# Adding the two halves of the attended values inside the transposing product on TensorE

## The chip, the core and the metric

The kernel runs on one core of a Trainium2 chip. The metric is device time of one launch in microseconds (us); the number given for a version is the median of its runs. The engines are named as in the profile: PE (TensorE's matrix products), PEld (its loads of the stationary operand), DVE (VectorE), ACT (ScalarE), POOL (GpSimd), SP (SyncE, which here only issues transfers).

## What is computed

Causal attention with a compressive memory over 4 batches of 8 heads, 576 tokens of 64 values each, feeds a layer of 8 experts of which each of the 2304 tokens goes to one.

```python
scores = scale * np.matmul(q, k.transpose(0, 1, 3, 2)); scores = np.where(causal, -1e9, scores)
a = np.exp(scores - scores.max(-1, keepdims=True)); a /= a.sum(-1, keepdims=True) + 1e-09
local = np.matmul(a, v)
mem_out = np.einsum('bhsd,bhde->bhse', phi(q), M_prev) / mem_norm
attn = g * mem_out + (1 - g) * local                 # B, H, S, D -> x of (B*S, H*D)
logits = x @ w_gate + modality_bias[modality_id]; e_idx = np.argmax(logits, axis=1)
for e in range(E):                                    # gate_w: the softmax value of the chosen expert
    out[mask_e] = gate_w[mask_e, None] * (np.maximum(x[mask_e] @ w1[e], 0.0) @ w2[e])
```

## The kernel before

**Precision.** Most matrix products are made of several in a reduced form of fp32 (`F32R`): an operand is split into a high and a low part, both of which are multiplied. The values `v` of a head lie in `vhl` as 64 columns of high parts beside 64 columns of low parts. With them as stationary operand (`av`, L707) the product of attention weights (`pth`, `ptl`) and values comes out in PSUM with 128 rows: 64 rows from the high parts and 64 from the low ones, one column a token. The attended value of a head is the sum of these halves.

**A head's way.** There are 32 heads, two to a pair, four pairs to a batch. `scores` (L641) gives the scores by TensorE, DVE masks them and takes the maximum (L669), ACT takes exponentials (L675); `ptrans` (L686) turns the result by TensorE transposes, ACT and DVE split it (L701, L703); `av` multiplies it with the values. The product lies in two PSUM banks, one of the first 128 tokens and one of the other 448. `memory` (L749) makes the memory's part of a pair by an fp32 product (L758).

**The sum of the halves, before.** For two of four heads (`NAVP = 2`) ACT copies both halves out (L733 to `ot`, L735 to `avt`), and POOL adds them in place (L744). For the other two ACT copies the lower half to `avt` (L738), and DVE adds the upper half from PSUM (L740). `ot` collects a pair, 64 rows a head. `combine` (L778) then brings tokens to the rows: five TensorE transposes of 128 columns a pair (L794), in two PSUM banks of three and two blocks, which DVE multiplies by the softmax's divisor (L797); POOL adds the memory's part (L801).

**What follows.** After each batch `gate` (L804) turns x and multiplies it with the gate's weights, `route` (L844) and `rank` (L925) choose experts on DVE and scatter the tokens' numbers to tables by POOL (L920). An expert's work is cut into slots of up to 256 or 384 tokens: `fetch` (L1002) reads the table by SP (L1009) and gathers rows by POOL (L1016); `slot` (L1032) turns them (L1042), splits them (L1050, L1052), and makes the first (L1064) and second product (L1086), with ACT (L1073) and DVE (L1075) between. The first three slots belong to the most frequent expert of batch 0 and run among the attention's work; slot 3 takes the tokens that this expert has left over, slot 4 more of them, and the others belong to a second expert, whose weights come by SP (L978) and are split by ACT (L985) and DVE (L989) once the attention's buffers are free.

**What sets the order.** Every step is an operation of a planner (`Plan`, L57) with an engine, an assumed duration and a place in the program's loop over heads. The planner goes through assumed time, and on each engine takes, of the steps that could begin within `WINDOW` ns of the earliest, the one with the lowest priority number; `EARLIER` shifts that number by stage and engine. Each engine runs its list strictly in this order. So a change of a duration, a window or a shift can move steps anywhere in the program.

Of the kernel before, what the change touches and what calls it, by code (L numbers as in the profile page):

```python
# [212 lines left out]
def kernel(  # L213
# [71 lines left out]
    NAVP = 2  # L285
# [12 lines left out]
    Plan.WINDOW = dict(zip(("PE", "ACT", "DVE", "POOL", "SP"), (0, 80, 85, 135, 75)))  # L298

    EARLIER = {  # L300
        "av": (-240.75, -614.75, 695.5, -837, 0),
        "bet": (0, 0, 0, 0, -366),
        "c": (-412, 0, 147.25, -2057.75, 0),
        "con": (0, 0, 0, 0, -347.25),
        "e": (222.75, -57, 141.25, 334, 0),
        "e1": (189.75, -20.5, -235.75, 614.5, 0),
        "e2": (186, 1704, -359, -1036.25, 0),
        "f": (0, 0, 1086.5, -188, 1075),
        "f1": (0, 0, -1054, -169.75, 612.5),
        "f2": (0, 0, 779.75, -443.5, -1457.5),  # L310
        "g": (-100, -1024, -307.5, 0, 1315),
        "k": (-396.5, -421.75, -279.25, 0, -133.25),
        "l": (0, 0, 33.25, 0, 0),
        "l2": (0, 0, 217.5, 0, 0),
        "ld": (0, 0, 0, 0, 204.5),
        "m": (418, 232, 747.75, 90.5, 0),
        "pt": (-80.25, 236.75, -864, 0, 0),
        "q": (-1459.5, 812.75, -363, 451.75, -995.5),
        "r": (85, -318.5, 476, 905, 0),
        "sc": (-53.75, 1043, 452, 0, 0),  # L320
        "tab": (0, 0, 0, 0, 200.25),
        "v": (0, 0, 0, -729, 0),
        "w": (0, 1380.25, 0, 286.25, -1110),
        "w1": (0, 179.25, 848.5, 0, 301.75),
        "w2": (0, -77, -1205.5, 0, 42.25),
        "warm": (-247, 0, 0, 0, 0),
# [58 lines left out]
    avt = ring(ap_, "avt", 1, [P, S])  # L385
    ot = ring(ap_, "ot", 2, [P, S])
# [12 lines left out]
    def setup():  # L399
# [13 lines left out]
        def pads():  # L413
# [293 lines left out]
    def av(d, prio):  # L707
# [21 lines left out]
        o_, a_ = ot[p % 2][64 * hh:64 * hh + 64], avt[0][64 * hh:64 * hh + 64]  # L729
# [47 lines left out]

    def combine(p, prio):  # L778
        b, h0 = divmod(p * 2, H)
        o_, m_, x_ = ot[p % 2], mt[0], xb[0]  # L780

        def e0():
            nc.vector.scalar_tensor_tensor(out=rnd, in0=nden[:, p % 4], scalar=1.0e-9,
# [541 lines left out]
    o = 0  # L1325
# [96 lines left out]
```

## Time and profile before

| | |
|---|---|
| median of three runs (lowest to highest) | 554.32 us (549.8 to 556.81) |
| the profiled execution: its own time | 550.81 us |
| its span, from first to last instruction | 549.1 us |
| busy share of the span: PE, PEld, DVE, ACT, POOL | 91%, 81%, 60%, 60%, 46% |
| mean granted TensorE clock | 0.966 of full speed |

Times within the profile count from the start of its span. A busy PE is not a PE at its peak: products overlap, and the length that the profile gives to one is several times the step to the next. The attention lasts until about 310 us; the change from the first expert to its leftovers and to the second one falls between 340 and 380, and the rest is the experts' products.

### The profile page before, as it was taken

To read this page: it belongs to the slowest core of one execution; us is meant where nothing else is said; L and a number is where in the kernel's file an instruction comes from. 1 tells how busy PE (TensorE), PEld (TensorE's weight loads), DVE (VectorE), ACT (ScalarE), POOL (GpSimd) and SP (SyncE) were. 2 spreads that over 40 slices of the span, in tenths; PEclk is the share of its full clock that TensorE was granted. 3 is DMA by queue.
4 is the path that set the end of the run, shared out by engine and by line. 5 is a ranking of instruction groups with operands and counts; after the bars stand their busy time and mean duration, and the time that the engine had idled before them with its cause. 6 is when DMAs were issued, how large, how long until landed. Compare 5 with 4: busy or idle time off the path is not lost. (4 is left out here: it accounts for less than half of the span.)

```text
span 549.1 us, 10861 instructions
## 1 busy us (share of the span) xinstructions
PE 497.9 (91%) x3420; PEld 445.1 (81%) x3420; DVE 330.5 (60%) x1066; ACT 329.0 (60%) x923; POOL 251.9 (46%) x257
## 2 busy tenths in 40 slices
PE   8898899987899889979898999769999999999992
PEld 8787888875787778869897898769897987989891
DVE  3788788897798988988878336653315512313010
ACT  4798898986999979979298244333325513222110
POOL 8462984656788768865761062350030004010100
PEclk9799899999899989989899999979999999999997
DMA  5888887988777997953740025474036203000100
GB/s 96 189 206 169 206 201 182 231 189 154 192 176 198 238 189 191 220 164 95 180 110 3 20 61 180 78 233 146 18 96 182 83 19 88 29 19 21 40 0 36
DMA packets 97101, 70.43 MB, mean 128 GB/s; under 512 B 73936, under 2 KB 74320, under 8 KB 97042
## 3 DMA queue, kind: packets, MB, share of 16 engines
q1 hardware_dynamic: 93330, 59.99, 45.2%
q0 software_dynamic: 3712, 9.72, 5.8%
q8 instruction: 28, 0.46, 0.4%
q14 instruction: 31, 0.25, 0.2%
HBM read 32.36 MB, written 10.16 MB: 77 GB/s over the span
## 5 line engine op out<-in xcount | busy, mean ns | idle before, releaser
L675 ACT ACTIVATE P<-P,nm 128x576 f32<-128x576 f32 (+4 forms) x160 | 88.5, 558 | 9.1 <-DVE nm L669 6.0
L1024 POOL DMA_INDIRECT out_dram<-osb,ids x19 | 18.9, 997 | 156.0 <-ACT osb L1093 115.3
L1064 PE MATMUL pa<-xh,w1h 128*128 128x256 f32 (+2 forms) x288 | 84.4, 293 | 2.6 <-ACT xh L1050 2.6
L1064 PE MATMUL pa<-xl,w1h 128*128 128x256 f32 (+2 forms) x288 | 83.4, 290 | 0.5 <-DVE xl L1052 0.3
L1064 PE MATMUL pa<-xh,w1l 128*128 128x256 f32 (+2 forms) x288 | 83.1, 288 | 0.0
L1075 DVE SCALAR_TENSOR_TENSOR hlo<-pa,hh 128x256 fp32r<-128x256 f32 (+1 forms) x72 | 29.8, 416 | 69.8 <-ACT hh L1073 69.7
L703 DVE TENSOR_TENSOR ptl<-pa,pth 128x512 fp32r<-128x512 f32 (+1 forms) x128 | 65.6, 564 | 3.0 <-ACT pth L701 2.4
L1073 ACT ACTIVATE hh<-pa 128x256 fp32r<-128x256 f32 (+1 forms) x80 | 29.0, 367 | 61.1 <-PE pa L1064 54.2
L669 DVE CUSTOM_DVE_ANT_0 P<-pa,maskw 128x320 f32<-128x320 f32 (+3 forms) x160 | 62.2, 427 | 4.2 <-PE pa L657 3.5
L684 PE MATMUL pa<-ident,P 128*128 128x128 f32 x320 | 57.6, 285 | 4.0 <-ACT P L675 3.7
L657 PE MATMUL pa<-ks,qs 128*128 128x192 f32 (+3 forms) x186 | 55.5, 329 | 5.9 <-ACT avt L735 2.9
L1086 PE MATMUL pa<-w2h,hh 128*128 128x512 f32 (+1 forms) x152 | 60.4, 397 | 0.0
L701 ACT ACTIVATE pth<-pa 128x512 fp32r<-128x512 f32 (+1 forms) x128 | 57.0, 511 | 5.0 <-PE pa L684 4.4
L1086 PE MATMUL pa<-w2l,hh 128*128 128x512 f32 (+1 forms) x152 | 59.6, 392 | 0.0
L1064 PEld LDWEIGHTS pa<-xh,w1h 128*128 128x128 f32 x288 | 55.6, 193 | 3.4 <-ACT xh L1050 2.9
L1064 PEld LDWEIGHTS pa<-xl,w1h 128*128 128x128 f32 x288 | 55.6, 193 | 1.2 <-DVE xl L1052 0.9
L1086 PE MATMUL pa<-w2h,hlo 128*128 128x512 f32 (+1 forms) x144 | 56.5, 392 | 0.0
L1064 PEld LDWEIGHTS pa<-xh,w1l 128*128 128x128 f32 x288 | 55.5, 193 | 0.0
L1093 ACT ACTIVATE osb<-pa,ids 128x512 f32<-128x512 f32 (+1 forms) x19 | 13.1, 687 | 68.4 <-PE pa L1086 63.1
L657 PE MATMUL pa<-kls,qs 128*128 128x192 f32 (+3 forms) x186 | 49.2, 295 | 0.4 <-DMA kls<-kl 0.4
L684 PEld LDWEIGHTS pa<-ident,P 128*128 128x128 f32 x320 | 40.4, 147 | 6.3 <-ACT P L675 6.0
L684 PE MATMUL pa<-swp,P 128*128 128x128 f32 x160 | 39.5, 287 | 6.1 <-DVE kl L617 2.5
(234 smaller groups left out, 1198.9 us busy)
## 6 DMA issues: line engine op xcount, KB each, us to landing
ks<-kh SPq DMA_DIRECT2D x62, 144.0 KB, 3.0
kls<-kl SPq DMA_DIRECT2D x62, 144.0 KB, 3.4
raw<-in_moe_w_dram SPq DMA_DIRECT2D x32, 256.0 KB, 3.5
qn<-in_q_dram SPq DMA_DIRECT2D x32, 144.0 KB, 4.3
kn<-in_k_dram SPq DMA_DIRECT2D x32, 144.0 KB, 4.2
qs<-qh SPq DMA_DIRECT2D x31, 144.0 KB, 2.6
qs<-ql SPq DMA_DIRECT2D x31, 144.0 KB, 2.7
vn<-in_v_dram SPq DMA_DIRECT2D x32, 128.0 KB, 3.0
```

What stands on the lines that cost most here:

```text
L657: nc.tensor.matmul(t.ap[0:m, o:o + z - x], lhsT=l[:, QS[j]:QE[j]], rhs=r[:, x:z], start=(i == 0), stop=(i == len(terms) - 1))
L669: nc.vector.tensor_tensor_reduce(out=pj[:, x:z], in0=t.ap[0:m, o:o + z - x], in1=mk, scale=-1.0, scalar=nm if x else 3.0e38, op0=ALU.add, ...
L675: g.op("ACT", act_ns(w, False, 2), lambda pj=pj, nm=nm, den=den, w=w: nc.scalar.activation(out=pj[:, 0:w], in_=pj[:, 0:w], func=AF.Exp, sc ...
L684: nc.tensor.transpose(t[:, o:o + P], prow[c % NPB][j][:, kb * P:(kb + 1) * P], swp if j == kb else ident)
L701: g.op("ACT", act_ns(n), lambda t=t, o=o, n=n: nc.scalar.activation(out=hi[:, o:o + n], in_=t.ap[:, 0:n], func=AF.Copy), r=[t], w=[("ph_", ...
L703: g.op("DVE", dve_ns(n), lambda t=t, o=o, n=n: nc.vector.tensor_tensor(out=lo[:, o:o + n], in0=t.ap[:, 0:n], in1=hi[:, o:o + n].bitcast(F3 ...
L1024: g.op("POOL", 1310, lambda: nc.gpsimd.indirect_dma_start(out=out[:, :], out_offset=bass.IndirectOffsetOnAxis(ap=ids[u % 4][0:m, t, 0:1].b ...
L1064: nc.tensor.matmul(hp.ap[:, 0:n_], lhsT=a[:, c, f * P:(f + 1) * P], rhs=x_[:, c, 0:n_], start=(n == 0), stop=(n == 3 * KC - 1))
L1073: g.op("ACT", act_ns(z - a), lambda f=f, hp=hp, i=i, a=a, z=z: nc.scalar.activation(out=hh[i][:, f, 0:z - a], in_=hp.ap[:, a:z], func=AF.R ...
L1075: g.op("DVE", dve_ns(z - a), lambda f=f, hp=hp, i=i, a=a, z=z: nc.vector.scalar_tensor_tensor(out=hlo[i][:, f, 0:z - a], in0=hp.ap[:, a:z] ...
L1086: nc.tensor.matmul(op.ap[0:m], lhsT=a[:, f, ts], rhs=w_[:, f], start=(y == 0 and n == 0), stop=(y == 3 and n == 5))
L1093: g.op("ACT", act_ns(512, True, 1), lambda t=t, op=op, oi=oi: nc.scalar.activation(out=osb[oi][0:m], in_=op.ap[0:m], func=AF.Copy, scale=i ...
```

## The change

The halves stay apart until `combine`. For every head ACT copies all 128 rows of the product out of PSUM in two instructions (128 and 448 columns) into one of three buffers `avt`; `ot`, POOL's sum and DVE's sum are gone. `combine` no longer transposes. For each head it multiplies, block by block of 128 tokens, `avt` as stationary operand with the constant `fold2`, 128 rows by 64 columns with two ones a column, 64 rows apart. Each of these products has the tokens in the rows and the summed halves in 64 columns; five blocks of a head fill 320 columns of one PSUM bank. The operands are plain fp32. DVE's scaling works by head instead of by group of blocks, in two instructions of 320 columns a pair where there were two of 384 and 256. `fold2` is made once at the start, by one POOL addition.

The diff also replaces the planner's numbers: `WINDOW`, nearly every row of `EARLIER` with own rows for the last five heads (`...9`) and for the three early slots (`ea` to `ec`, `fa` to `fc`), and the assumed durations of some routing steps.

```diff
-    NAVP = 2
+    NAV = 3
...
-    Plan.WINDOW = dict(zip(("PE", "ACT", "DVE", "POOL", "SP"), (0, 80, 85, 135, 75)))
+    Plan.WINDOW = dict(zip(("PE", "ACT", "DVE", "POOL", "SP"), (5, 90, 125, 115, 95)))
...
-        "av": (-240.75, -614.75, 695.5, -837, 0),
+        "av": (-88.25, -970.5, 0, 0, 0),
+        "av9": (-877, -854.25, 0, 0, 0),
...
-    avt = ring(ap_, "avt", 1, [P, S])
-    ot = ring(ap_, "ot", 2, [P, S])
+    avt = ring(ap_, "avt", NAV, [P, S])
+    fold2 = ap_.tile([P, D], F32, name="fold2")
...
+            gp.tensor_tensor(out=fold2, in0=ident[:, 0:D], in1=ident[:, D:P], op=ALU.add)
...
         for part, (t, a, z) in enumerate(((ta, 0, P), (tb, P, S))):
-            n, ko = z - a, ("ot", p % 2, hh, part)
-            if d % 4 < NAVP:
-                g.op("ACT", act_ns(n), lambda t=t, a=a, z=z, n=n: nc.scalar.activation(
-                    out=o_[:, a:z], in_=t.ap[0:64, 0:n], func=AF.Copy), r=[t], w=[ko], prio=prio)
...
-        if d % 4 < NAVP:
-            g.op("POOL", 1420, lambda: nc.gpsimd.tensor_tensor(out=o_, in0=o_, in1=a_, op=ALU.add),
-                 r=[("avt", 0), ("avt", 1)], w=[("ot", p % 2, hh, 0), ("ot", p % 2, hh, 1)], prio=prio)
+            g.op("ACT", act_ns(z - a), lambda t=t, a=a, z=z: nc.scalar.activation(
+                out=avt[d % NAV][:, a:z], in_=t.ap[:, 0:z - a], func=AF.Copy), r=[t], w=[("avt", d % NAV, part)], prio=prio)
...
-        for i, (a, z) in enumerate(PART):
-            t = Slot()
-
-            def e1(t=t, a=a, z=z):
-                for j in range(a, z):
-                    nc.tensor.transpose(t.ap[:, (j - a) * P:(j - a + 1) * P], o_[:, tok0(j):tok0(j) + P], ident)
...
+        for hh in range(2):
+            t, o = Slot(), (2 * p + hh) % NAV
+
+            def e1(t=t, o=o):
+                for j in range(NB):
+                    nc.tensor.matmul(t.ap[:, j * D:(j + 1) * D], lhsT=avt[o][:, tok0(j):tok0(j) + P], rhs=fold2, start=True, stop=True)
...
-        g.op("DVE", 1150, e0, w=["l0", "l1", "pr", "eb"], r=["basec", "modf", "iote", "tid"], prio=prio)
+        g.op("DVE", 1700, e0, w=["l0", "l1", "pr", "eb"], r=["basec", "modf", "iote", "tid"], prio=prio)
```

What this does to the order is seen at three places. Line numbers of the changed kernel differ; L743 is its copy out of PSUM, L793 its summing product, and L984, L1041, L1049, L1072, L1085 and L1092 are L985, L1042, L1050, L1073, L1086 and L1093 of before.

First, PE at the second pair of the second batch. Before, both groups of transposes of the pair stand together, between the turning of a later head's exponentials (L684) and a product with values (L715):

```order
L684 MATMUL pa5_95<-swp_80,P0_3_162 128x128
L684 MATMUL pa5_95<-ident_64,P0_4_163 128x128
L794 MATMUL pa6_96<-ident_64,ot1_175 128x128 x3
L794 MATMUL pa1_91<-ident_64,ot1_175 128x128 x2
L715 MATMUL pa2_92<-pth0_171,vhl0_142 128x128
```

Now the five summing products of the same pair's second head stand among the scores of later heads (L670, which was L657):

```order
L670 MATMUL pa3_93<-ks0_154,qs0_151 128x448
L670 MATMUL pa3_93<-kls0_157,qs0_151 128x448
L793 MATMUL pa1_91<-fold2_176,avt2_175 128x64 x5
L670 MATMUL pa6_96<-ks0_154,qs0_151 128x320
L670 MATMUL pa6_96<-kls0_157,qs0_151 128x320
```

One bundle a pair has become one bundle a head, and it no longer waits for a sum on DVE or POOL.

Second, ACT where the last batch is routed and the second expert's weights come in. `w1h1` are these weights' high parts, `raw` the buffers that they are loaded into, `xh0` the turned rows of slot 2, `hh0` its first product's result, `osb0` a finished block of outputs. Before:

```order
L877 ACTIVATE rex_128<-l0_125 128x40
L985 ACTIVATE w1h1_4292<-raw0_4304 128x512
L985 ACTIVATE w1h1_4292<-raw1_4305 128x512
L985 ACTIVATE w1h1_4292<-raw2_4306 128x512
L985 ACTIVATE w1h1_4292<-raw3_4307 128x512
L1093 ACTIVATE osb0_113<-pa7_97,ids1_103 128x512
L985 ACTIVATE w1h1_4292<-raw0_4304 128x512
L1093 ACTIVATE osb0_113<-pa0_90,ids1_103 128x512
L1050 ACTIVATE xh0_109<-pa6_96 128x512
L1050 ACTIVATE xh0_109<-pa3_93 128x512
```

Now:

```order
L1049 ACTIVATE xh0_109<-pa7_97 128x512
L1049 ACTIVATE xh0_109<-pa1_91 128x512
L1072 ACTIVATE hh0_111<-pa4_94 128x256
L876 ACTIVATE rex_128<-l0_125 128x40
L984 ACTIVATE w1h1_4297<-raw0_4309 128x512
L984 ACTIVATE w1h1_4297<-raw1_4310 128x512
L984 ACTIVATE w1h1_4297<-raw2_4311 128x512
L984 ACTIVATE w1h1_4297<-raw3_4312 128x512
L984 ACTIVATE w1h1_4297<-raw0_4309 128x512
L984 ACTIVATE w1h1_4297<-raw1_4310 128x512
L1092 ACTIVATE osb0_113<-pa0_90,ids1_103 128x512
L984 ACTIVATE w1h1_4297<-raw2_4311 128x512
```

The rows of slot 2 are split ahead of the routing instead of behind five copies of weights, and six copies of weights now come before the first block of outputs where there were four.

Third, PE around the transposes of slot 3's rows (`xg20`). Before, slot 2's first product is on both sides:

```order
L1064 MATMUL pa6_96<-xl0_110,w1h0_98 128x256
L1064 MATMUL pa6_96<-xh0_109,w1l0_99 128x256
L1042 MATMUL pa3_93<-ident_64,xg20_4300 128x128 x4
L1042 MATMUL pa2_92<-ident_64,xg20_4300 128x128 x4
L1064 MATMUL pa4_94<-xh0_109,w1h0_98 128x256
```

Now slot 2's second product is on both sides, and half of slot 4's transposes (`xg0`) come right behind:

```order
L1085 MATMUL pa4_94<-w2l0_101,hh0_111 128x512
L1085 MATMUL pa4_94<-w2h0_100,hlo0_112 128x512
L1041 MATMUL pa7_97<-ident_64,xg20_4305 128x128 x4
L1041 MATMUL pa1_91<-ident_64,xg20_4305 128x128 x4
L1041 MATMUL pa5_95<-ident_64,xg0_108 128x96 x4
L1085 MATMUL pa3_93<-w2h0_100,hh0_111 128x512
```

Between the routing's last product and these transposes PE has, before, 30 second products, the eight transposes of slot 2's rows and 84 of its first products. Now it has 84 first products and 60 second ones; the transposes of slot 2's rows and twelve of its first products stand ahead of the routing.

## Rows read from the trace of the kernel before

**Rows 1.** windows of three stages: length, busy us (count) of PE, PEld, DVE, ACT, POOL; clock

```profile
20.00:300.00 280.00, 250.18 (x1846) 223.96 (x1846) 236.44 (x806) 241.77 (x720) 188.85 (x168) 0.97 0.75 177
...
340.00:380.00 40.00, 32.34 (x220) 29.65 (x219) 24.08 (x69) 13.87 (x28) 14.20 (x14) 0.91 0.60 162
380.00:550.00 170.00, 158.43 (x940) 139.65 (x938) 42.07 (x96) 46.05 (x102) 22.95 (x23) 0.98 0.16 51
```

**Rows 2.** the same view, the first plain heads

```profile
20.00:80.00 60.00, 54.31 (x400) 49.14 (x399) 47.71 (x167) 54.09 (x164) 38.45 (x35) 0.97 0.86 200
```

**Rows 3.** groups by line of the copies and sums: xcount, busy us, mean ns

```profile
L701 ACT ACTIVATE pth<-pa 128x512 fp32r<-128x512 f32 x124 | 54.9, 511 | 3.8 <-PE pa L684 3.5
L735 ACT ACTIVATE avt<-pa 64x128 f32<-64x128 f32 (+1 forms) x32 | 13.0, 406 | 0.6
L740 DVE TENSOR_TENSOR ot<-pa,avt 64x128 f32<-64x128 f32 (+1 forms) x32 | 14.1, 446 | 4.5 <-ACT avt L738 3.9
L744 POOL TENSOR_TENSOR ot<-ot,avt 64x576 f32<-64x576 f32 x16 | 22.6, 1410 | 13.7 <-ACT avt L735 11.8 <-issue 1.7
```

**Rows 4.** TensorE's groups by form: the transposes removed, and the memory product

```profile
L758 PE MATMUL pa<-mz,ph 128*128 128x130 f32 x160 | 23.1, 287 | 1.4 <-POOL ph L603 1.3
L794 PE MATMUL pa<-ident,ot 128*128 128x128 f32 x80 | 14.4, 304 | 4.0 <-DVE ot L740 2.3 <-POOL ot L744 1.6
```

**Rows 5.** TensorE's timeline: start us, length us, count; the steps of both kinds

```profile
156.50 0.83 PE L758 MATMUL pa<-mz,ph 128*128 128x130 f32 x6
157.17 0.27 PE L684 MATMUL pa<-ident,P 128*128 128x128 f32 x1
...
163.57 0.49 PE L684 MATMUL pa<-ident,P 128*128 128x128 f32 x3
```

**Rows 6.** loads of the stationary operand, ns min/median/max, by columns and kind

```profile
L826 PEld LDWEIGHTS pa<-kh,wgs x32: 93/96/147, 88.9 to 330.9; 128*16 128x16 f32 x32
L684 PEld LDWEIGHTS pa<-ident,P x320: 137/141/230, 12.3 to 303.6; 128*128 128x128 f32 x160
L758 PEld LDWEIGHTS pa<-mz,ph x160: 186/191/338, 23.2 to 319.0; 128*128 128x128 f32 x160
```

**Rows 7.** TensorE's timeline: eleven products of 192 columns in a row, first and last

```profile
405.87 0.28 PE L1064 MATMUL pa<-xh,w1h 128*128 128x192 f32 x1
...
406.99 0.27 PE L1064 MATMUL pa<-xl,w1h 128*128 128x192 f32 x1
```

**Rows 8.** ScalarE's waits between 20 and 300: us, times, longest

```profile
ACT P L675 <- DVE nm L669: 6.0, 8, 1.8
...
ACT ot L733 <- PE pa L715: 3.9, 5, 1.8
...
ACT avt L738 <- PE pa L720: 0.3, 2, 0.2
```

**Rows 9.** TensorE's timeline at the switch of experts

```profile
337.74 0.48 PE L1086 MATMUL pa<-w2h,hh 128*128 128x512 f32 x1
...
344.82 1.04 PE L1042 MATMUL pa<-ident,xg 128*128 128x128 f32 x8
348.48 0.39 PE L1064 MATMUL pa<-xh,w1h 128*128 128x256 f32 x1 [2.62 <-ACT xh L1050]
...
358.60 0.28 PE L1064 MATMUL pa<-xh,w1l 128*128 128x256 f32 x1
362.13 0.45 PE L1042 MATMUL pa<-ident,xg 128*128 128x128 f32 x1 [3.25 <-issue]
364.03 1.75 PE L1042 MATMUL pa<-ident,xg 128*128 128x128 f32 x7 [1.46 <-DMA xg<-x_dram,ids]
```

**Rows 10.** timelines of ScalarE and of SyncE's queue at the switch

```profile
347.83 1.08 ACT L1050 ACTIVATE xh<-pa 128x512 fp32r<-128x512 f32 x2
...
353.92 3.29 SPq L1009 DMA_DIRECT2D idr<-tbl  x6
```

**Rows 11.** windows: the clock behind the wait at the switch

```profile
361.20:368.20 7.00, 4.62 (x21) 4.35 (x22) 4.75 (x11) 3.42 (x8) 4.74 (x5) 0.51 0.84 223
```

More of the change, by code (lines that the diff above doesn't have):

```diff
@@ new lines @@
+        "f2": (0, 0, 1405.75, 324.25, -1170.75),
+        "fa": (0, 0, 1004, -525.75, 769.75),
+        "fb": (0, 0, 889.5, -170, 1614),
+        "fc": (0, 0, 1611.25, -141.5, 835),
+        "g": (-355.25, -741, -623, 0, 1487.75),
+        "g9": (-289.75, -411.25, -116.5, 0, 540.75),
+        "k": (-443.5, 86.75, -694.75, 0, -16),
+        "l": (0, 0, -77.75, 0, 0),
+        "l2": (0, 0, 995.5, 0, 0),
+        "ld": (0, 0, 0, 0, 188.5),
+        "m": (908.5, 373, 499.25, -179.25, 0),
+        "m9": (530.25, -235.25, 1030.5, -397.25, 0),
@@ new lines @@
+        "pt": (-148.25, 426.5, -910.25, 0, 0),
+        "pt9": (-728, -199.25, -608.75, 0, 0),
+        "q": (-1373.25, 735, -677.75, 188.5, -1128.25),
+        "r": (77.25, 105.5, 894.25, 785.5, 0),
+        "r9": (-295, 80.5, 1077, 683.5, 0),
+        "sc": (38.25, 837.25, 187, 0, 0),
+        "sc9": (-689.25, 1038.25, 582.5, 0, 0),
+        "tab": (0, 0, 0, 0, 247.25),
+        "v": (0, 0, 0, -876.75, 0),
+        "w": (0, 2206.5, 0, -304.25, -1222),
+        "w1": (0, -46.5, 1143, 0, 11),
+        "w2": (0, -422, -871.5, 0, 335),
@@ L327 @@
+        "warm": (-433, 0, 0, 0, 0),
     }
@@ L779, in combine @@
         b, h0 = divmod(p * 2, H)
[L780 removed]
+        m_, x_ = mt[0], xb[0]
         def e0():
@@ L1195, with at @@
         m, odd = divmod(n, 2)
+        def at(stage):
+            return stage + ("9" if n >= NH - 5 else "")
         if 0 <= n < NH:
-            av(n, ("av", n))
+            av(n, (at("av"), n))
         if 0 <= n + 1 < NH:
-            ptrans(n + 1, ("pt", n))
+            ptrans(n + 1, (at("pt"), n))
         if 0 <= n + 2 < NH:
-            scores(n + 2, ("sc", n))
+            scores(n + 2, (at("sc"), n))
         if odd:
@@ L1224 @@
                         if b < EARLY:
-                            fetch(g, b, start(b), 2, ["nst", ("perm", 0)], ("f", n), (b + 1) * S)
-                            slot(g, b, 0, 2, ("e", n))
+                            fetch(g, b, start(b), 2, ["nst", ("perm", 0)], ("f" + "abc"[b], n), (b + 1) * S)
+                            slot(g, b, 0, 2, ("e" + "abc"[b], n))
             if 0 <= m < NPR:
@@ L1229 @@
                     load_m(m // NP + 1, ("ld", n))
-                memory(m, ("m", n))
+                memory(m, (at("m"), n))
             if 0 <= m + 2 < NPR:
@@ L1234 @@
     mctx = ExitStack()
-    attn = [o for o in g.ops if o.stage not in ("r", "w", "f", "e")]
+    attn = [o for o in g.ops if o.stage[:1] not in set("rwfe")]
     def swap():
@@ L1318 @@
     u = EARLY
-    route(g, B - 1, ("r", NH))
+    route(g, B - 1, ("r9", NH))
     steps = leftovers()
-    for i, ns in enumerate((2200, 1400, 2600, 2600)):
+    for i, ns in enumerate((2800, 1750, 2600, 2600)):
         g.op("DVE", ns, lambda: next(steps), r=["basec", "thr", "swap"] + (["left"] if i else []),
```

66 lines of the change are left out of this document (21 added, 45 removed).

## The prediction, made before the changed kernel ran

> **What bounds the kernel now.** I read the windows by stage first: between 20 and 300 us the attention keeps three engines nearly equally busy, PE 250.2, ACT 241.8 and DVE 236.4 of 280 us, POOL 188.9 [rows 1]; behind 380 PE alone is busy. In the first plain heads ACT has 54.1 of 60 us [rows 2]. PE's 250 is not its load: a group's length holds the way through the array besides its place in the queue. Six products of the memory begin at 156.50 and what follows them at 157.17, so one takes a step of 0.112 us, though a lone one is given 0.27 or so [rows 5]. At 0.11 us a step the 1846 products of the stage need some 203 us, an estimate from that step, and PE stands 77 us, mostly in gaps too short to show. So in the attention ACT, with 86%, and DVE, with 84%, stand closest to their limit, and PE is third, with 73%. The waits of ACT there sum to 35.3 us in 13 rows, of which seven rows of the attention's own copies, from 3.9 to 0.3, wait for PE, 13.5 us together [rows 8]. Then I read the switch of experts, from 340 to 380: PE has 32.3 of 40 us at a clock of 0.91 [rows 1].
>
> **The sum of the halves, removed.** Of the three groups of copies one goes: L735, 32 instructions, 13.0 us of ACT. The others keep their columns and get 128 rows, which costs nothing: L701's 512 columns by 128 rows take 511 ns on average [rows 3], and the copies of 64 rows are no cheaper by the column. DVE loses L740, 14.1 us, POOL loses L744, 22.6 us [rows 3]. PE no longer waits for these sums ahead of L794, 4.0 us in all [rows 4].
>
> **The product, added.** L794's 80 transposes go. Three transposes in a row take 0.49 us and a lone one 0.27, so a step is 0.11 [rows 5], and they held 8.8 us of PE's queue. The new products are fp32 and not transposes, as the memory's are. The memory has 16 pairs of five blocks, 80 products, but the trace shows 160 instructions [rows 4]: each fp32 product is two. So 160 new products are 320 instructions. No row shows one with 64 columns. The lower end goes by columns: 130 cost 0.112, so 64 cost half of it, 0.055, 17.6 us together and 8.8 more than now. The upper end goes by the load of the stationary operand. A load takes 96 ns with 16 columns, 141 with 128 columns of a transpose, and 191 with 128 columns of the memory's product [rows 6]; and products of 192 columns, which would take 0.08 by columns alone, keep a step of 0.112 with such loads (ten steps from 405.87 to 406.99) [rows 7]. I take that: 320 times 0.11 is 35.2 us, 26.4 more than now, 0.83 us a head. It is the nearer row, since the loads of the memory's product are the very kind that the new ones need, and 64 columns cannot hide them.
>
> The rows of the memory's product say 0.224 us for a whole fp32 product of 130 columns, which either price explains. The Trainium skill, FP8 and Floating Point Precision, section TensorE Precision Notes, says that true fp32 makes four passes through the array; counted in passes of columns alone, a product of 64 columns costs about what a transpose of 128 does. It would make the added time the lower end, and it is the second rival below.
>
> **What the attention gains or loses.** If ACT stays the limit at the same fullness of 0.864, 228.8 us of work need 264.9 instead of 280: minus 15. DVE gets 222.3, less in proportion, so it doesn't take over. PE would need 229 of 265, 87%, as full as ACT. Not all of its added time is hidden. Of ACT's waits 38% are for PE (13.5 of 35.3), and I charge this share of 26.4: plus 10. That share is a choice; its ends are nothing, and all of it. The attention comes out 5 us shorter.
>
> The other edits cost nothing that shows. DVE's scaling has 640 columns a pair in two instructions, as before. `fold2` is one POOL instruction at the start, where PE is busy with warming. The new waits are those of a summing product on ACT's two copies, behind which stand the scores and turnings of later heads in PE's queue; three buffers give a head's copy the time of two more heads before its buffer is wanted.
>
> **The switch.** Here only the order changes. Before, from 337.74 to 344.82, PE has 30 second products, 0.236 us each, then the transposes of slot 2's rows, 2.62 us of waiting for ACT, and 84 first products to 358.60; then it waits 3.25 and 1.46 us for slot 3's rows [rows 9]. ACT splits slot 2's rows only at 347.83, behind five copies of weights and an output; slot 3's rows are late because SP reads the table only at 353.92, when the scatter has landed [rows 10]. Behind the waits the clock is at 0.51, its lower level of 1.2 GHz, for 7 us [rows 11]. In the new order slot 2's rows are split ahead of the weights, so the 2.62 goes, and PE has 84 first products (0.12 us each) and 60 second ones, some 24 us of cover, while the scatter, the table and the gather run, instead of 17. What is moved ahead of the routing, eight transposes (0.9 us) and twelve products (1.4 us), delays the routing by as much. By the time that slot 3's rows arrive PE has thus done 30 second products (7.1 us) and 12 first ones (1.4 us) more, 8.5 us, and they arrive 2.3 us later: minus 6. Against it stand two new waits: half of slot 4's transposes come right behind slot 3's, so that their gather holds up PE, and in ACT's list six copies of weights come in a row, each with a load to wait for.
>
> **Sum.** The profiled execution took 550.8 us; minus 5 and minus 6 gives 540. The median of the three runs shown is 554.3, 0.6% above that execution, so 540 lies 2.0% below the one and 2.6% below the other; 2% is about what a measurement of this kernel can tell from no change.
>
> **Rivals.**
> *The order doesn't pay at the switch.* ACT's copies of weights wait for loads, and slot 2's results stand behind them: the ninth copy's load is queued on SP behind the reads of the table, which come at 353.92 now [rows 10], and the last results of slot 2 stand behind that copy. Then PE finds fewer second products ready than its order holds, and the 6 us stay lost: 546, or up to 553 if the attention gains nothing either. For it speaks that ACT waited for such loads before; against it, that the rows themselves come as late in either case and that the first products need no more than free PSUM banks.
>
> *The product is cheap.* If columns decide, the added time is 8.8 us and not 26.4; charged at 38% it is 3, the attention gains 12, and with the switch the time is 533, down to 526 if the clock's drops in the attention, which come behind waits, become fewer. Against it speak the loads of 191 ns.
>
> *TensorE becomes the bound* and the kernel is slower. With 0.83 us a head added, PE's queue needs 229 us plus its real gaps for the array's delay; those 77 us of standing are perhaps not free but the delay between each product and its reader, and then all 26.4 us lie on the path and the savings of ACT and DVE, which then wait for PE, count for nothing: 550.8 plus 26.4 less 6, 571. It decides from the point where more than 15 of the 26.4 us lie on the path. For it speaks that PE already shows the most busy time of all engines [rows 1]; against it, that ACT is as full, and that the new products come in bundles of ten instructions that wait for little.
>
> **Chances.** The forecast, between 532 and 546: 0.45. The cheap product: 0.22. No gain at the switch: 0.22. TensorE as bound: 0.11. The predicted time is the forecast's, 540. The range leaves out the last rival and the outermost of the third: 526 to 555. Faster by over 2% takes in two thirds of the forecast and the cheap product, 0.52; within 2% the rest of the forecast and the third case, 0.37; slower by over 2% the last rival, 0.11.
>
> **What would show it.** The group of the new products should have 320 instructions, loads of about 190 ns, and a step of 0.11 us inside a bundle: 1.1 us for a head's five products. With a step of 0.06 the cheap product is right. Between 20 and 300 us ACT's copies L733, L735 and L738 should be one group of 64 instructions and 26 us. The last summing product should end a few us earlier than the last L794, which starts at about 310. At the switch no wait of PE over 2 us should stand between slot 2's transposes and its first products, and slot 3's transposes should begin with slot 2's second product under way. I'd be wrong most if PE's waits in the attention became waits for nothing but its own queue, with ACT's busy share falling by more than the 13 us of work that it lost.

## The result, and the profile after

The changed kernel takes 555.22 us (median of 20 runs, 551.47 to 559.23) against 550.21 us for the kernel before (median of 20 runs beside them, 546.04 to 556.98). The ratio is 1.0111, 95% interval 1.0085 to 1.0137: slower by 1.1%, some 6 us, where 540 us was forecast. A ratio leaves out every run over 1.5% above the fastest of its kernel, while the medians are of all runs, so the two need not agree: the two medians lie 5.0 us apart. The profiled execution has a span of 550.8 us.

First the windows by stage of the changed kernel, to be read against [rows 1], with the same columns:

```profile
20.00:300.00 280.00, 257.85 (x2018) 241.04 (x2018) 223.64 (x771) 225.29 (x689) 165.83 (x151) 0.98 0.72 177
...
340.00:380.00 40.00, 36.45 (x223) 31.42 (x222) 25.96 (x89) 14.95 (x32) 11.96 (x10) 0.96 0.54 137
```

In the same 280 us ACT has 16.5 us less to do than before, DVE 12.8 and POOL 23.0 less. ACT's share fell from 86% to 80%. Where its saved time went is in its list of waits between 20 and 300 us, the counterpart of [rows 8]: 17 rows that sum to 53.1 us, where 13 rows had 35.3. These are the first five:

```profile
ACT P L688 <- DVE nm L682: 9.5, 14, 2.0
ACT avt L743 <- PE pa L733: 9.2, 10, 1.9
ACT avt L743 <- PE pa L728: 7.2, 9, 3.6
ACT pth L714 <- PE pa L697: 5.6, 9, 1.7
ACT kh L628 <- PE pa L567: 3.7, 6, 1.4
```

So 17.8 us more of waiting stand against 16.5 us less of work.

The last bundle of summing products nevertheless begins earlier than the last transposes did, as the prediction had named for a sign. First the kernel before, then the changed one:

```profile
309.96 0.71 PE L794 MATMUL pa<-ident,ot 128*128 128x128 f32 x5
```

```profile
306.92 1.22 PE L793 MATMUL pa<-fold,avt 128*128 128x64 f32 x10
```

But less of other work stands ahead of it. These are the first products (L1064, now L1063) and the second ones (L1086, now L1085) of the slots up to there, before and then now; the first number in brackets counts them:

```profile
0.00:310.00 310.00, 13.05 (x96) 12.46 (x96) 0.96 0.71 167
0.00:310.00 310.00, 6.22 (x24) 4.29 (x24) 0.96 0.71 167
```

```profile
0.00:307.00 307.00, 9.82 (x72) 8.88 (x72) 0.97 0.70 169
0.00:307.00 307.00, 0.00 (x0) 0.00 (x0) 0.97 0.70 169
```

In the new order 24 first and 24 second products, some 8.5 us of PE's queue at the prediction's steps of 0.12 and 0.236 us, have moved behind the last bundle. So the earlier bundle is no sign that the attention gained.

Next the groups by line of the copies, of the products and of their loads, the counterpart of [rows 3, 4, 6], and the timeline of one head's products:

```profile
L743 ACT ACTIVATE avt<-pa 128x128 f32<-128x128 f32 x64 | 26.1, 408 | 19.1 <-PE pa L733 9.6 <-PE pa L728 9.4
...
L793 PE MATMUL pa<-fold,avt 128*128 128x64 f32 x320 | 40.2, 271 | 1.4 <-ACT avt L743 1.4
...
L793 PEld LDWEIGHTS pa<-fold,avt x320: 186/192/192, 20.5 to 307.8; 128*128 128x128 f32 x160
...
111.10 1.23 PE L793 MATMUL pa<-fold,avt 128*128 128x64 f32 x10
112.16 1.33 PE L757 MATMUL pa<-mz,ph 128*128 128x130 f32 x10
```

The 64 copies of 128 rows take 26.1 us, and 160 products are 320 instructions with loads of 192 ns. From 111.10 to 112.16 ten instructions, one head's five products, take 1.06 us of PE's queue.

Last the switch of experts, to be read against [rows 9 to 11]: PE's timeline, ACT's, and the clock behind PE's wait.

```profile
346.34 0.27 PE L897 MATMUL pa<-ohb,ones 128*128 128x8 bf16 x5
...
368.15 0.50 PE L1085 MATMUL pa<-w2h,hh 128*128 128x512 f32 x1 [3.37 <-ACT hh L1072]
```

```profile
358.13 0.63 ACT L984 ACTIVATE w1h<-raw 128x512 fp32r<-128x512 f32 x1 [3.87 <-DMA raw<-in_moe_w_dram]
...
367.20 0.63 ACT L984 ACTIVATE w2h<-raw 128x512 fp32r<-128x512 f32 x1 [5.30 <-DMA raw<-in_moe_w_dram]
367.73 0.64 ACT L1072 ACTIVATE hh<-pa 128x256 fp32r<-128x256 f32 x2
```

```profile
369.00:376.00 7.00, 7.00 (x28) 5.61 (x27) 3.82 (x7) 1.88 (x3) 3.36 (x3) 0.76 0.88 276
```

PE's waits of 2.62 and 3.25 us for the rows of slots 2 and 3 are gone; one of 3.37 us for a result of slot 2 is there instead. From the routing's last products to the end of the span it is now 550.8 less 346.3, that is 204.5 us. Before, the routing ended just ahead of 337.74 [rows 9], which leaves 211.4. So the end of the kernel gained some 7 us, and the part before it got 8.6 us longer, of which 2.3 us are the work that the prediction counts as moved ahead of the routing.

### The profile page after: what moved, and what is told of

Read it like the earlier page. It is cut to its first block, busy times and chain, and to the rows that moved or that the text cites. A ratio compares the mean times of both kernels' runs of the same rounds, so it can differ in the third digit from the quotient of the medians.

```text
span 550.8 us, 11259 instructions
## 1 busy us (share of the span) xinstructions
PE 511.1 (93%) x3660; PEld 467.8 (85%) x3660; DVE 317.7 (58%) x1034; ACT 312.6 (57%) x891; POOL 230.9 (42%) x242
## 5 line engine op out<-in xcount | busy, mean ns | idle before, releaser
L688 ACT ACTIVATE P<-P,nm 128x192 f32<-128x192 f32 (+4 forms) x160 | 88.7, 559 | 13.4 <-DVE nm L682 13.0
L1063 PE MATMUL pa<-xh,w1h 128*128 128x256 f32 (+2 forms) x288 | 83.5, 290 | 0.0
L1063 PE MATMUL pa<-xl,w1h 128*128 128x256 f32 (+2 forms) x288 | 82.4, 286 | 0.1
L1063 PE MATMUL pa<-xh,w1l 128*128 128x256 f32 (+2 forms) x288 | 82.3, 286 | 0.0
L1085 PE MATMUL pa<-w2h,hh 128*128 128x512 f32 (+1 forms) x152 | 60.5, 398 | 3.4 <-ACT hh L1072 3.4
L670 PE MATMUL pa<-ks,qs 128*128 128x192 f32 (+4 forms) x186 | 58.1, 336 | 5.7 <-DMA qs<-ql 3.0
L1072 ACT ACTIVATE hh<-pa 128x256 fp32r<-128x256 f32 (+1 forms) x80 | 28.8, 366 | 60.4 <-PE pa L1063 52.7
L1085 PE MATMUL pa<-w2l,hh 128*128 128x512 f32 (+1 forms) x152 | 60.2, 396 | 0.0
L1085 PE MATMUL pa<-w2h,hlo 128*128 128x512 f32 (+1 forms) x144 | 57.2, 397 | 0.0
L697 PE MATMUL pa<-ident,P 128*128 128x128 f32 x320 | 54.9, 278 | 2.2 <-DMA qs<-qh 1.9
L1063 PEld LDWEIGHTS pa<-xl,w1h 128*128 128x128 f32 x288 | 54.6, 190 | 0.7 <-DVE xl L1051 0.3
L1063 PEld LDWEIGHTS pa<-xh,w1h 128*128 128x128 f32 x288 | 54.6, 189 | 0.7
L1063 PEld LDWEIGHTS pa<-xh,w1l 128*128 128x128 f32 x288 | 54.6, 190 | 0.0
L1092 ACT ACTIVATE osb<-pa,ids 128x512 f32<-128x512 f32 (+1 forms) x19 | 13.1, 689 | 71.3 <-PE pa L1085 67.5
L670 PE MATMUL pa<-kls,qs 128*128 128x192 f32 (+4 forms) x186 | 50.5, 301 | 0.6 <-DMA kls<-kl 0.6
L670 PEld LDWEIGHTS pa<-ks,qs 128*128 128x128 f32 (+1 forms) x186 | 34.9, 187 | 8.7 <-issue 3.1
```

Of the source, the lines that this page charges most:

```text
L670: nc.tensor.matmul(t.ap[0:m, o:o + z - x], lhsT=l[:, QS[j]:QE[j]], rhs=r[:, x:z], start=(i == 0), stop=(i == len(terms) - 1))
L688: g.op("ACT", act_ns(w, False, 2), lambda pj=pj, nm=nm, den=den, w=w: nc.scalar.activation(out=pj[:, 0:w], in_=pj[:, 0:w], func=AF.Exp, sc ...
L697: nc.tensor.transpose(t[:, o:o + P], prow[c % NPB][j][:, kb * P:(kb + 1) * P], swp if j == kb else ident)
L1063: nc.tensor.matmul(hp.ap[:, 0:n_], lhsT=a[:, c, f * P:(f + 1) * P], rhs=x_[:, c, 0:n_], start=(n == 0), stop=(n == 3 * KC - 1))
L1072: g.op("ACT", act_ns(z - a), lambda f=f, hp=hp, i=i, a=a, z=z: nc.scalar.activation(out=hh[i][:, f, 0:z - a], in_=hp.ap[:, a:z], func=AF.R ...
L1085: nc.tensor.matmul(op.ap[0:m], lhsT=a[:, f, ts], rhs=w_[:, f], start=(y == 0 and n == 0), stop=(y == 3 and n == 5))
```

## The experiments

**Half and twice the products, in the new order.** Theory A: the products lie almost wholly on the path, the third rival. Theory B: 38% of them do, as forecast, and the new order loses the rest.

```diff
-    avt = ring(ap_, "avt", NAV, [P, S])
-    fold2 = ap_.tile([P, D], F32, name="fold2")
+    avt = ring(ap_, "avt", NAV, [P, S], F32R)
+    fold2 = ap_.tile([P, D], F32R, name="fold2")
```

> The changed kernel with avt and fold2 in the reduced form of fp32, so that each summing product is one instruction instead of two; the attended values are rounded, which changes the output. 160 instructions of 0.112 us go, 17.9 us of TensorE's queue; the order and all else stay. Theory A (the products lie almost wholly on the path): 14 to 18 us less than the changed kernel, ratio to the kernel before 0.978 to 0.985. Theory B (they are hidden as forecast, 38% on the path, and the new order loses the rest): 7 us less, ratio about 0.998.

Measured: 553.78 us, ratio to the kernel before 1.0027 (0.9976 to 1.0078). Of 17.9 us less on PE (160 instructions of 0.112) some 4.6 show against the changed kernel, a quarter. The mean granted clock is lower as well, 0.960 over these ten runs against 0.972 over the 20 of the changed kernel, so a part of the saving may have gone to the clock; no run separates the two.

```diff
-                for j in range(NB):
+                for j in 2 * list(range(NB)):
```

> The changed kernel with every bundle of summing products issued twice, into the same place: 320 more instructions, 35.8 us of TensorE's queue. Theory A: 29 to 36 us more than the changed kernel, ratio to the kernel before 1.063 to 1.077. Theory B: 14 us more, ratio about 1.036.

Measured: 579.34 us, ratio 1.054 (1.0459 to 1.0621). Of 35.8 us more some 23.6 show, two thirds. The price is bent, as if the products filled gaps first and lay on the path after that. Theory A falls, since then the first halving would have shown 18 us.

**The new sum with the old numbers, and the old order without a sum.** In the first run the changed kernel gets `WINDOW`, `EARLIER` and the durations of before. In the second the kernel before leaves out the sum: ACT copies one half for each head, and no addition is there.

> The changed sum with the planner's windows, shifts and assumed durations of the kernel before. Theory A: the attention is as long as in the changed kernel, and what the new order gave at the switch (7 us) is lost: 558 to 563, ratio 1.015 to 1.025. Theory B: the attention gets some 12 us shorter, less 7 at the switch: 549 to 551, ratio 0.998 to 1.003.

Measured: 609.14 us, ratio 1.1071 (1.1014 to 1.1128).

> The kernel before without the sum: ACT copies the upper 64 rows alone, for all heads, and the lower half is left out of the output; POOL's and DVE's sums and 13.0 us of ACT are gone, nothing is added. If removing them is worth what was forecast: 15 us less than before, ratio 0.973. If they were hidden anyway: ratio 0.995 to 1.0, and the summing products would have had no gain to set against.

Measured: 563.62 us, ratio 1.0256 (1.0206 to 1.0307). Both miss what either theory expected. Work was taken away, and the kernel got 2.6% slower: with other operations the planner finds another order, and that outweighs the work. Neither run says what the sum costs. The tests of the sum behind them kept the order fixed.

**Each part by itself, in the old order.** In the next runs the planner gets the same operations with the same durations as before, so that it finds the same order; in the traces of these runs the rows of PE, ACT, DVE and POOL stand as before, but for those left out or replaced. An operation that a test takes away stays in its list and issues nothing:

```diff
-                g.op("DVE", dve_ns(n), lambda t=t, a=a, z=z, n=n: nc.vector.tensor_tensor(
-                    out=o_[:, a:z], in0=t.ap[0:64, 0:n], in1=avt[0][0:64, a:z], op=ALU.add),
-                     r=[t, ("avt", part)], w=[ko], prio=prio)
+                g.op("DVE", dve_ns(n), lambda: None, r=[t, ("avt", part)], w=[ko], prio=prio)
```

The first run does this to the second copies, to DVE's and to POOL's additions.

> The kernel before with every instruction in its old place in each engine's row, but without the sum: ScalarE copies one 64-row half for each head (64 copies instead of 96), VectorE's 32 additions and GpSimd's 16 are not issued, and the transposes carry that one half (so the other half of each attended value is missing from the output). It removes 13.0 us of ScalarE, 14.1 of VectorE and 22.6 of GpSimd and adds nothing. The prediction's step (ScalarE is the limit, and its saving shows at the same fullness): 15 us less, ratio to the kernel before 0.973. The rival that has grown out of the first four runs (the attention is a chain through five rows of work in which no engine is the limit, so that a removed copy or addition mostly becomes a wait): ratio 0.990 to 1.000.

Measured: 542.47 us, ratio 0.9865 (0.9778 to 0.9951): 7.4 us, half of the forecast. The second run has the whole change of the sum in the old places; `ot` has three buffers of 128 rows here, and the products read it.

> The whole change of the sum (128-row copies on ScalarE, products with the two ones a column, scaling by head), but with every instruction in the place that the kernel before gave it; the places of the removed instructions stay empty. If the products lie on the path almost wholly and the removed work is worth its 15 us, 26.4 less 15: ratio 1.015 to 1.02. If the removed work is worth little and a part of the products' 26.4 us is hidden (26 to 66 hundredths of it, by the runs with half and twice the products): 7 to 17 us more, ratio 1.01 to 1.03. If the new order is what the changed kernel loses, and the sum itself gains as forecast, ratio 0.98.

Measured: 550.53 us, ratio 1.0005 (0.9954 to 1.0056). The removed work and the new products cancel. The products cost 1.0005 less 0.9865, that is 0.014 or 7.7 us of their 26.4, with a half width of 5.6. PE's waits between 20 and 300 us sum to 29.6 us in the run before this one and to 16.5 in this one; that fits products of which 13 us fill waits of PE. Then the same with `F32R` for `ot` and `fold2`:

> The run above with the products in the narrower 32-bit type that TensorE multiplies in one instruction in place of two: 160 instructions of it instead of 320, about 18 us of TensorE less, in the same places. If the products lie on the path wholly: 3 hundredths below the run above. If a quarter of the saving shows, as it did in the new order: 0.008 below it. Against the kernel before: below 0.99 only if the removed work is worth what was forecast.

Measured: 545.42 us, ratio 0.9915 (0.9867 to 0.9963). Half of the instructions gone are worth 0.009 or 5.0 us of 17.9, about the share that the whole of them has. Last, in the new order, one product of 320 columns for five of 64 (with `avt` and `fold2` as `F32R`):

```diff
-                for j in range(NB):
-                    nc.tensor.matmul(t.ap[:, j * D:(j + 1) * D], lhsT=avt[o][:, tok0(j):tok0(j) + P], rhs=fold2, start=True, stop=True)
+                nc.tensor.matmul(t.ap[:, 0:NB * D], lhsT=avt[o][:, tok0(NB - 1):S], rhs=avt[o][:, 0:NB * D], start=True, stop=True)
```

> The changed kernel in its own order, with one product of 320 columns for each head in place of the five summing products (its output is then not the sum): TensorE's price of the sum falls from 36 us to about 5. If the products lie on the path almost wholly, 25 to 30 us less than the changed kernel, ratio to the kernel before 0.96. If only the first 18 us of them showed a quarter, as in the run with half the products, 5 to 9 us less: ratio 0.995 to 1.00. The second would say that the order itself holds the attention where it is, whatever the sum costs.

Measured: 729.6 us, ratio 1.3275. The time tells nothing of the products. With other values in x the routing chooses other experts, and what fits no slot goes through the loop behind the slots, one tile of tokens a pass. Its groups by line in this run, first products and second ones:

```profile
L1381 PE MATMUL pa<-lxt,w1r 128*128 128x128 f32 x320 | 47.4, 322 | 3.7 <-ACT lxt L1378 3.7
L1387 PE MATMUL pa<-w2r,lht 128*128 128x512 f32 x80 | 35.2, 592 | 0.0
```

That is ten passes of 32 and 8 products; the changed kernel has no row of these lines. Ahead of that loop the rows of PE are those of the changed kernel, and the attention can be read. Here are the last of the 32 products and the window of the attention:

```profile
311.79 0.31 PE L792 MATMUL pa<-avt 128*128 128x320 f32 x1
```

```profile
20.00:300.00 280.00, 241.98 (x1722) 217.85 (x1721) 225.36 (x753) 217.86 (x671) 165.56 (x152) 0.93 0.76 177
```

The last bundle began at 306.92 in the changed kernel. So in this one profile the attention is no shorter with the products nearly gone, as the second expectation says, and the clock is lower, 0.93 against 0.98.

**Which engine's work was worth it.** The kernel before again in its own order. First without the additions of POOL, as below, and of DVE, as above, with all copies:

```diff
-            g.op("POOL", 1420, lambda: nc.gpsimd.tensor_tensor(out=o_, in0=o_, in1=a_, op=ALU.add),
+            g.op("POOL", 1420, lambda: None,
```

> The kernel before in its own order, without VectorE's 32 additions and GpSimd's 16 (14.1 and 22.6 us), but with all 96 copies of ScalarE; the output then lacks the lower half of each attended value. The prediction's step, ScalarE as the limit of the attention, expects nothing: ratio 1.00. If the attention is a chain through the rows of all engines, in which a sum that comes late holds up the transposes behind it, most of the 0.0135 of the run without any of the sum should be here: ratio 0.988 to 0.993.

Measured: 549.13 us, ratio 0.9968 (0.9925 to 1.001), without one of the eleven runs, which took 2617 us. Then without the second copies, with all additions:

```diff
-                g.op("ACT", act_ns(n), lambda t=t, a=a, z=z, n=n: nc.scalar.activation(
-                    out=a_[:, a:z], in_=t.ap[64:P, 0:n], func=AF.Copy), r=[t], w=[("avt", part)], prio=prio)
+                g.op("ACT", act_ns(n), lambda: None, r=[t], w=[("avt", part)], prio=prio)
```

> The kernel before in its own order, without ScalarE's 32 second copies (13.0 us), the very copies that the change saves, but with all additions; GpSimd's 16 add zeros in place of the half that was not copied, so half of the heads lack it in the output. The prediction's step expects 15 us less: ratio 0.973. The chain expects little: ratio 0.995 to 1.00.

Measured: 548.33 us, ratio 0.9957 (0.9922 to 0.9992). The same window, 20 to 300 us, in three kernels (the sum gone, the additions gone, the copies gone):

```profile
20.00:300.00 280.00, 249.01 (x1872) 226.67 (x1871) 227.29 (x783) 229.50 (x699) 166.80 (x152) 0.97 0.75 177
```

```profile
20.00:300.00 280.00, 249.05 (x1864) 224.87 (x1863) 226.18 (x777) 241.98 (x728) 165.74 (x152) 0.97 0.75 177
```

```profile
20.00:300.00 280.00, 247.75 (x1853) 224.56 (x1852) 237.10 (x808) 230.43 (x694) 188.76 (x168) 0.97 0.75 177
```

With the copies gone ACT does 230.4 us of work instead of 241.8 [rows 1] in the same 280 us, and the time falls by 2.4 us, with a half width of 1.9. ACT's waits in this window sum to 47.2 us, where they were 35.3 [rows 8]. That refutes the prediction's step: ACT was not the limit. Nor are DVE and POOL, with 1.8 us, which the interval doesn't tell from nothing. The two parts together make 4.1 us, and both at once 7.4, equal within the intervals.

**The order, by planner numbers.** The kernel with the products in the old order, with the changed kernel's rows of `EARLIER` from slot 2 on (`ec`, `fc`, `r9`, `l`, `l2`, `w1`, `w2`, `e1`, `e2`, `f1`, `f2`) and two of its assumed durations; then the same with `F32R`.

> The whole change of the sum with the order before in the attention (the first 1830 of TensorE's 3065 rows stand where they stood) and the changed kernel's planner numbers from slot 2 on, so that the switch of experts is ordered as in the changed kernel. If the changed kernel's new order of the attention is what cost it its gain, and the switch gives its 5 to 7 us by itself: ratio to the kernel before 0.987 to 0.992. If the gain at the switch can only be had with the new order of the attention, which brings the work forward for it: ratio 1.00, as in the run with the products in the old order. If the old order of the attention only looked better by chance: 1.01.

> The run above with the products in the narrower 32-bit type, half as many instructions, about 18 us of TensorE less. By what half the products gave in the old order it should lie 0.009 below the run above: 0.978 to 0.984, faster than both kernels. If the products stand in gaps here: as the run above.

Measured: 554.15 us, ratio 1.0065 (1.0024 to 1.0105), and 548.38 us, ratio 0.9897 (0.982 to 0.9974). The first misses, the second is what the cheap products gave without these numbers. The order that came out was a third one, and in it the stretch behind the routing takes 215 us, longer than in either kernel (in the second run, 546.6 of span less 331.05). So this tells only that the switch's order can't be had by its numbers alone.

**The order, row by row.** In the changed kernel the planner now follows a written list for each engine, and only the PSUM banks are still chosen by it:

```diff
-                lst = [o for o in lst if o.alloc is None or rooms[o.alloc.n] is not None and self.may(o.alloc)]
+                lst = [o for o in lst if o is self.ops[FORCED[e][pos[e]]] and (o.alloc is None or rooms[o.alloc.n] is not None)]
```

The lists are mixtures: the old order up to the last summing product and the new one behind it, with both types of products; the new order with one load moved; the new order until head 23 and the old one from there.

> The changed kernel with its rows put in an order by hand: up to the last summing product each engine follows the order before (with the products in the places of the transposes), and from there the changed kernel's own order, so that the switch of experts is the same row for row. If the new order of the attention is what the changed kernel loses, and the switch's gain of 6.4 us (its stretch from the routing's last product to the end took 204.1 to 205.7 us in three profiles of the new order against 209.4 to 212.9 in six of the old one) belongs to the switch alone: the ratio of the products in the old order, 1.0005, less 0.012, that is 0.989. If that gain comes from work left over by a longer attention, and is merely the other side of it: 1.00. If the last splice's 1.0065 tells what such a mixture costs: 1.005 or above.

Measured: 547.29 us, ratio 0.993 (0.9883 to 0.9977).

> The run above with the products in the narrower 32-bit type, half as many instructions. By the step between the two runs in the old order, 0.009 below the run above: 0.980 if the switch's gain belongs to the switch, 0.991 if it doesn't.

Measured: 536.97 us, ratio 0.9766 (0.9706 to 0.9827), the fastest of all, 2.3% below the kernel before and 3.4% below the changed one. The same computation as in the changed kernel, in another order, is 1.8% faster (0.993 against 1.0111, a difference of 0.018 with a half width of 0.005; with the PSUM banks chosen anew). The cheap products round the attended values. The cores' line and the routing's last products of the first of these runs, then of the products in the old order throughout:

```profile
core 0: 547.4 us, clock 0.969
...
342.12 0.27 PE L902 MATMUL pa<-ohb,ones 128*128 128x8 bf16 x5
```

```profile
core 0: 550.5 us, clock 0.970
...
340.76 0.27 PE L896 MATMUL pa<-ohb,ones 128*128 128x8 bf16 x5
```

The stretch behind the routing is 205.3 us with the new switch and 209.7 with the old one, so the switch's gain goes with the switch. (The expectation counts from the last of the five products, which makes each 0.4 us shorter.)

> The changed kernel in its own order but for one place: SyncE's load of the values of a later pair (three transfers, 1.99 us from 238.17 in the profile) goes behind the two copies of q that TensorE waits 2.96 us for at 246.07, with its clock at the lower level behind it. If this wait is what the new order costs: the wait shrinks to about 1 us, the lower clock behind it goes, 3 to 4 us less, ratio 1.004. If the loss is spread over the last batch: within 0.002 of the changed kernel's 1.011.

Measured: 554.31 us, ratio 1.0103 (1.0033 to 1.0172). The wait and what hangs on it are gone: the window from 246 to 250 us in the changed kernel, and in this run:

```profile
246.00:250.00 4.00, 3.93 (x17) 3.83 (x18) 2.01 (x10) 1.09 (x3) 0.00 (x0) 0.57 0.58 185
```

```profile
246.00:250.00 4.00, 4.00 (x34) 3.80 (x34) 2.57 (x12) 2.16 (x7) 2.51 (x3) 1.00 0.39 104
```

PE does 34 products there instead of 17, at a clock of 1.00 instead of 0.57, and the kernel is not measurably faster. The interval has room for the 3 to 4 us of the first expectation, so this doesn't show that the wait was worth nothing.

> The changed kernel with the new order until the product with values of head 23 (three of four batches), and from there the order before for whatever is left. If the new order loses in the last batch alone, as the profiles look (heads 24 to 31 took 67.3 us without the slots' products in the new order, 61.3 in the old one, while head 23 ended at 230.4 and 233.3): the ratio of the products in the old order, 1.00. If it loses before that as well: 1.01 or above, since the gain at the switch is gone too.

Measured: 556.25 us, ratio 1.016 (1.0092 to 1.0228). Against the old order throughout, 1.0005, the new order of the first three batches and the seam behind it cost 0.0155 or 8.5 us, with a half width of 4.7. Whether they are lost ahead of the seam or behind it isn't shown. The last products with values of head 23, in this run and then in the products in the old order:

```profile
229.63 0.93 PE L738 MATMUL pa<-ptl,vhl 128*128 128x448 f32 x5
```

```profile
232.34 0.94 PE L721 MATMUL pa<-ptl,vhl 128*128 128x448 f32 x5
```

So this profile is 2.7 us ahead at head 23 and loses behind it: its last summing products begin at 312.56, against 311.68 in the old order. The profile of the changed kernel, too, is ahead there (229.39) and behind at the routing (346.34 against 340.76). But single profiles of the same rows scatter by more than what is sought. The last twenty summing products begin at 311.68 and 310.75 in two kernels, and at 316.77 in a third, whose TensorE rows up to there are the same (the products in the old order, the first run of this group, and the splice by planner numbers):

```profile
311.68 2.34 PE L792 MATMUL pa<-fold,ot 128*128 128x64 f32 x20
```

```profile
310.75 2.34 PE L798 MATMUL pa<-fold,avt 128*128 128x64 f32 x20
```

```profile
316.77 2.34 PE L795 MATMUL pa<-fold,ot 128*128 128x64 f32 x20
```

## Why the prediction was wrong

The runs give each term of the sum a measured value. The first four differences add up to the result by themselves; 0.001 is taken as 0.55 us.

| term | forecast | measured | from |
|---|---|---|---|
| additions and copies removed | -15 | -7.4 (half width 4.8) | sum gone, old order |
| products added | +10 of 26.4 | +7.7 (5.6) | products in the old order less sum gone |
| new order of the attention | no term | +10.0 (3.0) | changed kernel less the exact splice |
| new order of the switch | -6 | -4.1 (3.8) | exact splice less products in the old order |
| sum | -11 | +6.1 (1.4) | |

By the medians of all runs the four differences are -7.4, +8.0, +6.9 and -2.5, together +5.0. The signs are the same; the last two terms are smaller.

**The step that failed** is "If ACT stays the limit at the same fullness of 0.864, 228.8 us of work need 264.9 instead of 280: minus 15". ACT wasn't the limit. Its copies by themselves gave 2.4 us of 13.0, and in the changed kernel its waits grew by what its work shrank. I took the highest busy share for a limit where three engines stand between 84% and 90% and each follows its own fixed list. The share was also an average of two stages. The kernel before, up to 245 us and from there to the routing:

```profile
20.00:245.00 225.00, 199.00 (x1440) 175.93 (x1439) 192.17 (x654) 200.81 (x599) 157.45 (x140) 0.97 0.83 197
245.00:335.00 90.00, 86.18 (x652) 79.92 (x651) 58.69 (x192) 55.01 (x159) 40.95 (x36) 0.98 0.33 85
```

From 245 us on, with slots' products among the last heads, PE has 86.2 of 90 us and ACT 55.0, 61%: there ACT can't be the limit. Up to 245 ACT has 89%, and that its waits grew when its copies went fits a stage made of hand-overs from row to row, in which work taken from one engine becomes, for the most part, a wait on the same engine. That is a reading of the sums; no run follows a single hand-over. The Trainium skill, Perfetto Trace Analysis, section Identifying the Most-Contended Engine, advises to find the engine with the highest occupancy (for TensorE it goes by the busy share of its loads, among others) and to improve it first; ACT's 86% was the highest by that measure, against 80% for the loads. The runs here don't bear it out for this stage: its relief by 13.0 us was worth 2.4.

**The term that was missing** is the new order of the attention. The prediction costed the new planner numbers at the switch, where they could be read, and at nothing in the 300 us ahead of it. They cost 10 us there, more than any other term. Two things that could explain it are excluded. It is not the price that the planner assumes for the products: it counts 570 ns a head, where 1.06 us are taken (at 111.10 above), but with the cheap products, which take half of that, the new order is behind the old one by as much (1.0027 against 0.9915; with the full products 1.0111 against 1.0005). And it is not, for the most part, the one long wait that only the new order has: at the end of its interval the run without it gains 4 us. Where the 10 us are lost stays open. With the new order up to head 23 alone the kernel is slow already, but the profiles of both kernels with that order are ahead there and behind later, and single profiles scatter by more than the loss at any one place.

**Right was the price of the products:** 320 instructions, loads of 192 ns, a step of 0.106 to 0.112 us, 1.1 us a head. So the second rival, the cheap product, is out, and with it the count by columns alone that the prediction worked out from the four passes: ten instructions with 64 columns hold PE's queue for 1.06 us, 0.106 each, and the memory's, with 130, take nearly the same step of 0.112 us [rows 5]. The Trainium skill, FP8 and Floating Point Precision, section TensorE Precision Notes, gives true fp32 four passes; the trace here doesn't agree with pricing them by columns alone. The share of the added time that lies on the path was forecast as 38%, and 29% was measured in the old order. It isn't fixed: in the old order it is near 30% from none to half the products and on to the whole, in the new order 66% from the whole to the double. That the forecast was near is partly luck. Its 38% leaves out a row of the slots, in which ACT waits for PE as well:

```profile
ACT hh L1073 <- PE pa L1064: 5.6, 4, 1.8
```

With it 19.1 of 35.3 us, 54%, of ACT's waits are for PE, and by the same rule the term would have been 14 us.

**Right was the switch.** The waits for slots 2 and 3 went, and the stretch behind the routing became 4 to 7 us shorter (204.5 against 211.4, and 205.3 against 209.7). Against the 8.5 us that the prediction counted there, less the 2.3 us of work that moved ahead of the routing, the forecast was 6; the exact splice gives 4.1 and, with the cheap products, 8.2 (0.9766 against 0.9915), with a half width of about 4. The first rival's mechanism is there as well, as rows 358.13 to 367.73 show: ACT waits 5.30 us for a load of weights, slot 2's results stand behind that copy, and PE waits 3.37 us for them. The gain at the switch came in spite of it.

**The third rival** named the right side for the wrong reason. From 245 us on PE is by far the fullest engine, as it said of the whole attention. But not all 26.4 us of the products lay on the path, and the removed work did not count for nothing; the order ahead of the switch made the kernel slower.

## What to carry to other kernels

Where several engines are nearly equally full and each runs a fixed list, ask of a piece of work who waits for it, not whose share is highest; here half of the forecast saving showed. A change that also replaces the order is two changes: run the new computation in the old order first, with emptied places, and only then the new order, stage by stage. Here the fastest version of the whole sum was neither kernel but the new computation with the old order in one stage and the new order in the other (0.993, and 0.9766 with the cheap products, which round).

## What was not expected of the hardware

Removing a wait of 2.96 us of TensorE, and with it a stretch of 4 us at a clock of 0.57, changed the time by nothing that 5 runs can tell (1.0103 against 1.0111; up to 4 us would lie within the interval). And the same rows of TensorE, up to the last summing product, took 5 to 6 us longer in one profile than in two others (316.77 against 311.68 and 310.75), which is as much as the effects under study; only medians of several runs told them apart. Time and granted clock go together from run to run: of the 20 runs of the changed kernel the fastest, 551.47 us, has a mean clock of 0.982, the slowest, 559.23, one of 0.966. Which of the two sets the other isn't shown.
